# Float16 copies as 32-bit words on ScalarE, and a new written order, in a fused sliding-window attention and token-mixing kernel

## The chip, the cores and the metric

The kernel runs on one core of a Trainium2 chip. The metric is the device time of one execution in microseconds. Three runs of the kernel before took 137.32, 137.8 and 139.23 us; their median is 137.8.

A core has TensorE (PE), which multiplies matrices and writes its results to PSUM; VectorE (DVE) and ScalarE (ACT), which read PSUM and write SBUF; GpSimd (POOL), which here mostly issues the loads; and SyncE (SP), which here issues stores. The engines run side by side and wait for each other through semaphores.

## The reference

Eight batches, eight heads, 576 positions, head size 64. First causal attention over a window of 128 keys with a slope per head, then, with the heads laid side by side (512 columns), a mixing step over the tokens:

```python
scores = scale * np.matmul(q, k.transpose(0, 1, 3, 2))
rel = pos[:, None] - pos[None, :]
bias = slopes[:, None, None] * (-np.abs(rel))[None, :, :]
scores = np.where((rel >= 0) & (rel < 128), scores + bias[None], -1e9)
attn = softmax(scores)                       # over the keys
x = np.matmul(attn, v)                       # then (batch, 576, 512)
wq, wk = x @ w_q, x @ w_k                    # 512 -> 64
W_tok = np.einsum('bsd,btd->bst', wq, wk) / 8
mixed = np.einsum('bst,btd->bsd', W_tok, x)
out = np.maximum(mixed, 0.0) @ w_out         # float32
```

## The kernel before

Every piece of work is an operation with a name, a batch and a part. The long text `ORDER` lists all of them; the kernel issues them in exactly that order, and each word says on which engine the operation runs (`P`, `A`, `D`, `G`, `S` for PE, ACT, DVE, POOL, SP) and, for PE, which PSUM banks it writes. PSUM is used as four pairs of banks. Each engine executes its own operations strictly in the order of the text, so an operation that waits holds up all that is behind it on that engine.

Per batch b:

- `Lq`, `Lk`, `Lv`, `Lt` load q, k, v and the last 64 rows of q and k, converting to float16; POOL issues them. K comes in four parts of 128 rows (128 KB each as float16), Q of batches 1 to 4 in one load of 512 KB, Q of batches 5 to 7 in four loads of 128 KB, V in five parts. Three buffers hold K, two Q, four V, so a load waits until the batch that had its buffer is through. Batch 0's first blocks come in float32 through ACT and SP (`LF`).
- `TQ`, `TK`, `TT`, `TJ`, `TF` transpose q and k on PE by a product with an identity; `ETQ`, `ETK`, `ETT`, `EJ`, `EF` copy the result from PSUM to SBUF (tile qkT), on DVE or ACT as the order says.
- `QK b.g.u` computes the scores of 128 keys for half of the heads; `EXP` takes their exponential on ACT into tile pt (64 of them in all); `MUL` on DVE multiplies by the precomputed exp(bias), zero outside the window.
- `PV b.t` multiplies with V, which has a column of ones beside each head, so that the sums of the exponentials come with it; `RC` and `X` on DVE take the reciprocal and scale (tile x). `ones` sets that column in each of the four V buffers (tile vt) before the first load.

Two batches form a group for the mixing step: `XT`, `XTT` transpose x on PE and `EXT`, `EXTT` copy it out (tiles xT, xTt); `WQ`, `WK`, `WT`, `G` are products, evicted with conversion by `EWQ`, `EWK`, `EWT`, `EG`; `MX` and `RM`, `RMT` give the rectified mix (tile rm); `OUT` multiplies with w_out, `EO` copies to tile osb, `DO` stores.

`WM.i` are matmuls on a zeroed tile (tile warm) whose results nobody reads; `WARM` gives how many each one has. `bias`, `wmc`, `zeros`, `pads`, `ident`, `idh` prepare constants.

All copies from PSUM without arithmetic go through one helper, `cp`, in lines 250 to 254: `nc.scalar.copy` on ACT (line 252), `nc.vector.tensor_copy` on DVE (line 254). So in the profile all of these stand under L252 and L254, all products under L240, all transposes under L243; L657 is `EXP`, L672 `MUL`, L723 `RC`, L733 `X`, L886 and L888 are `RM` on ACT and DVE. Loads of K, Q and V are L367, L371 (L379 for batches 5 to 7) and L393.

Of the kernel before, what the change touches and what calls it, by code (L numbers as in the profile page):

```python
# [17 lines left out]
H = 8  # L18
# [36 lines left out]
EXP0.0.1:A QK0.2.1:P3 EJ0.1.1:D QK0.2.0:P2 QK0.1.1:P1 EXP0.2.1:A MUL0.0:D TQ1:P0 EXP0.2.0:A
Lv0.2:G QK0.1.0:P3 Lt0:G ETQ1:D EXP0.1.0:A TK1.0:P2 ETK1.0:D EXP0.1.1:A Lv1.0:G MUL0.2:D
WM.2:P01 QK1.1.1:P2 QK1.1.0:P3 QK1.0.1:P1 EXP1.1.1:A Lv1.1:G QK1.0.0:P0 MUL0.1:D EXP1.1.0:A
Lq2.0:G TK1.1:P2 ETK1.1:D EXP1.0.1:A Lk2.3:G PV0.0:P3 QK1.2.1:P2 RC0.0:D Lk2.2:G X0.0:D
EXP1.0.0:A PV0.1:P1 MUL1.1:D PV0.2:P3 Lv1.2:G EXP1.2.1:A QK1.2.0:P0 Lv0.3:G RC0.1:D EXP1.2.0:A
X0.1:D TT0:P2 RC0.2:D Lv1.3:G TJ0.3.1:P1 X0.2:D ETT0:A XT0.0:P00 ETT1:A MUL1.0:D Lk2.0:G  # L60
EJ0.3.1:A WM.3:P01 QK1.3.0:P2 Lv0.4:G EXP1.3.0:A EXT0.0:D PV1.0:P1 QK0.3.1:P3 RC1.0:D PV1.1:P0
X1.0:D EXP0.3.1:A QK0.3.0:P2 MUL1.2:D QK1.3.1:P1 EXP0.3.0:A TQ2:P3 Lk2.1:G RC1.1:D EXP1.3.1:A
MUL0.3:D Lv1.4:G ETQ2:A WM.4:P21 TK2.1:P1 X1.1:D Lt1:G ETK2.1:D PV1.2:P2 XT1.0:P00 RC1.2:D
PV0.3:P3 X1.2:D Lw1:G QK2.2.1:P1 MUL1.3:D Lk3.1:G EXP2.2.1:A Lw0:G RC0.3:D WM.5:P01 PV1.3:P2
EXT1.0:A X0.3:D Lq3.0:G PV0.4:P01 RC1.3:D X1.3:D TK2.0:P3 QK2.2.0:P1 Lv2.0:G RC0.4:D PV1.4:P00
ETK2.0:D EXP2.2.0:A XT1.1:P20 Lk3.0:G RC1.4:D X0.4:D QK2.0.0:P3 EXT1.1:D XT0.1:P21 EXP2.0.0:A
Lk3.3:G QK2.0.1:P1 X1.4:D EXT0.1:D QK2.1.1:P0 Lk3.2:G EXP2.0.1:A TT2:P3 QK2.1.0:P2 ETT2:D
Lv2.1:G EXP2.1.1:A ETT3:D WK0:P10 MUL2.0:D Lv2.2:G EXP2.1.0:A XTT0:P0 QK2.3.0:P3 EXTT0:D
WQ0:P11 Lv2.3:G EWK0:A MUL2.1:D EXP2.3.0:A QK2.3.1:P0 TQ3:P2 Lq4.0:G MUL2.2:D EXP2.3.1:A Lwo0:G
WT0:P10 ETQ3:D PV2.0:P0 EWT0:A Lwo1:G TK3.0:P3 ETK3.0:A G0:P10 RC2.0:D Lk4.1:G X2.0:D MUL2.3:D  # L70
EWQ0:A Lk4.0:G TK3.1:P3 EG0:A QK3.0.0:P0 EXP3.0.0:A Lv3.0:G ETK3.1:D MX0.0:P1 QK3.0.1:P2
RM0.0:D MX0.1:P3 EXP3.0.1:A Lv3.1:G MX0.3:P0 Lq5.01:G RM0.3:D RM0.1:A PV2.1:P1 QK3.1.0:P2
# [24 lines left out]
QK6.0.1:P3 ETT7:D DO2.1:S QK6.0.0:P1 ETQ7:D Lv6.3:G EXP6.0.1:A PV5.4:P20 DO0.1:S OUT3.2:P21
DO1.3:S Lv6.4:G EXP6.0.0:A RC5.4:D DO1.0:S MUL6.1:D QK6.3.0:P0 Lv7.0:G DO0.0:S PV5.3:P3
EXP6.3.0:A OUT3.1:P10 X5.4:D Lv7.4:G RC5.3:D EO3.2:A X5.3:D Lv7.2:G QK6.3.1:P0 EO3.1:A
QK7.1.0:P2 MUL6.0:D MX2.4:P3 EXP6.3.1:A XT5.1:P11 Lv7.1:G OUT2.0:P10 RMT2:D EXP7.1.0:A EXT5.1:D  # L100
TK7.1:P0 QK7.0.0:P3 EO2.0:A XTT4:P2 MUL6.2:D OUT3.0:P11 EXTT4:A EXP7.0.0:A ETK7.1:D WT4:P10
QK7.1.1:P2 MUL6.3:D EWT4:A QK7.0.1:P3 PV6.0:P0 EXP7.1.1:A WK4:P10 RC6.0:D X6.0:D EXP7.0.1:A
PV6.1:P2 MUL7.1:D PV6.2:P0 EO3.0:A QK7.3.0:P3 EWK4:A RC6.2:D DO3.0:S RC6.1:D WQ4:P11 X6.2:D
EXP7.3.0:A DO1.1:S X6.1:D PV6.4:P10 DO1.2:S EWQ4:A QK7.3.1:P0 DO2.3:S RC6.4:D QK7.2.1:P2 X6.4:D
QK7.2.0:P3 EXP7.3.1:A DO0.3:S MUL7.0:D G4:P11 DO1.4:S EXP7.2.1:A DO2.2:S MUL7.3:D PV6.3:P0
DO2.0:S EG4:A OUT3.4:P10 DO3.1:S EXP7.2.0:A RC6.3:D X6.3:D PV7.4:P11 EO3.4:A MX4.4:P2 MX4.1:P3
# [53 lines left out]
def kernel(  # L160
# [75 lines left out]
    def hold(i):  # L236
        held.append(i.ins)
# [12 lines left out]
    def cp(eng, out_ap, in_ap):  # L250
        if eng == "ACT":
            hold(nc.scalar.copy(out_ap, in_ap))  # L252
        else:
            hold(nc.vector.tensor_copy(out=out_ap, in_=in_ap))  # L254
# [820 lines left out]
```

## Time and profile before

| | |
|---|---|
| median of three runs | 137.8 us (137.32 to 139.23) |
| the profiled execution, its own time | 137.96 us |
| its span on the core | 135.9 us |
| mean granted TensorE clock | 0.982 |
| busy: PE / DVE / ACT / POOL | 122.4 / 114.2 / 107.4 / 86.4 us |
| first exponential starts, last one ends | 10.10, 105.42 us |
| last load issued by POOL | 93.2 us |

Each line of the views gives an engine, the kernel's line, the operation and its tiles as output<-input with shapes, then counts and times. Matmul ends are modelled in this profile, so a PE that is busy all the time may still contain short waits. "Idle before" is time in which an engine waited ahead of an instruction, with the engine and line that ended the wait.

### The profile page before, as it was taken

How to read it: one execution, taken by the hardware profiler on the slowest of the kernel's cores; microseconds unless marked ns; L12 is line 12 of the kernel's file. 1: busy time of each engine (PE TensorE's matmuls, PEld its weight loads, DVE VectorE, ACT ScalarE, POOL GpSimd, SP SyncE). 2: the span in 40 equal slices, each digit the busy share in tenths (PEclk: the TensorE clock that was granted, in tenths of full speed). 3: DMA queues.
4: the chain of work that ended last, by engine and by line, in shares of the span. 5: the costliest groups of instructions: out<-in, count | busy, mean ns of one | idle time of the engine just before them, and what ended most of it. 6: DMA issues, size and time to landing. Idle time of an engine off the chain costs nothing.

```text
span 135.9 us, 5044 instructions
## 1 busy us (share of the span) xinstructions
PE 122.4 (90%) x2169; PEld 78.1 (57%) x2169; DVE 114.2 (84%) x197; ACT 107.4 (79%) x145; POOL 86.4 (64%) x108
## 2 busy tenths in 40 slices
PE   6778778888999799999999999999999999999960
PEld 2356555765676476575566575565685576634430
DVE  5746699998999999998999999699999999557720
ACT  2579699985999999998999999999999953276040
POOL 7997979698989857999999999998000000000000
PEclk9997799999999999999999999999999999999997
DMA  4999999999999999999999999999999800958794
GB/s 91 214 176 171 157 154 181 164 159 151 148 164 160 197 186 154 157 154 157 155 157 158 152 150 155 154 192 265 226 244 376 306 20 0 299 187 312 236 378 138
DMA packets 105414, 24.97 MB, mean 184 GB/s; under 512 B 95536, under 2 KB 100912, under 8 KB 105392
## 3 DMA queue, kind: packets, MB, share of 16 engines
q0 software_dynamic: 96832, 14.42, 149.6%
q1 hardware_dynamic: 6688, 9.44, 20.6%
q10 hardware_dynamic: 1872, 0.79, 2.2%
q8 instruction: 17, 0.28, 0.8%
q14 instruction: 5, 0.04, 0.1%
HBM read 29.62 MB, written 9.44 MB: 287 GB/s over the span
## 4 chain that ended last, share of the span: by engine, by line
PE 57%; DMA 17%; DVE 8%; POOL 6%; ACT 6%; issue 3%; ACTq 0%; POOLq 0%; DVEq 0%
PE pair L240 48%; DMA natk<-in_k_dram 11%; PE pair L243 9%; DMA natq<-in_q_dram 6%; POOL natk L367 3%; ACT pt L657 3%; DVE pt L672 3%; DVE qkT L254 2%; DVE rm L888 1%; POOL vt L393 1%; POOL natq L371 1%; DVE x L733 1%; ACT rm L886 1%; ACT wqT L252 0%; ACT gs L252 0%
## 5 line engine op out<-in xcount | busy, mean ns | idle before, releaser
L657 ACT ACTIVATE pt<-pair 128x1024 f16<-128x1024 f32 x64 | 63.0, 1038 | 6.5 <-PE pair L240 5.9
L672 DVE TENSOR_TENSOR pt<-pt,bias 128x2048 f16<-128x2048 f16 x32 | 38.5, 1216 | 0.4 <-ACT pt L657 0.3
L393 POOL DMA_DIRECT2D vt<-in_v_dram x40 | 35.3, 968 | 2.2 <-DMA natk<-in_k_dram 1.0
L240 PE MATMUL pair<-wout_sb,rm 128*128 128x512 f16 (+1 forms) x132 | 31.7, 373 | 0.0
L367 POOL DMA_DIRECT2D natk<-in_k_dram x31 | 28.6, 946 | 1.7 <-DMA natq<-in_q_dram 1.4
L240 PE MATMUL pair<-qkT 64*128 64x256 f16 (+2 forms) x320 | 23.0, 256 | 1.3 <-DVE qkT L254 0.8
L240 PE MATMUL pair<-vt,pt 128*128 128x65 f16 (+1 forms) x576 | 22.1, 194 | 1.8 <-DVE rm L888 0.5
L240 PEld LDWEIGHTS <-pt 128*128 128x128 f16 (+1 forms) x576 | 19.2, 100 | 7.7 <-issue 3.4
L254 DVE COPY qkT<-pair 128x1024 f16<-128x1024 f16 (+2 forms) x27 | 19.3, 735 | 4.0 <-PE pair L243 3.9
L733 DVE TENSOR_TENSOR x<-pair,inv 128x512 f16<-128x512 f32 x32 | 21.8, 690 | 0.9
L252 ACT COPY osb<-pair 128x512 f32<-128x512 f32 (+1 forms) x24 | 14.0, 596 | 10.4 <-PE pair L240 5.1
L240 PEld LDWEIGHTS <-rm 128*128 128x128 f16 x132 | 11.4, 97 | 12.0 <-issue 2.2
L240 PEld LDWEIGHTS <-qkT 64*128 64x128 f16 x320 | 11.4, 95 | 8.9 <-issue 5.5
L254 DVE COPY osb<-pair 128x512 f32<-128x512 f32 (+1 forms) x13 | 8.7, 667 | 5.1 <-PE pair L240 5.1
L379 POOL DMA_DIRECT2D natq<-in_q_dram x12 | 11.5, 995 | 2.2 <-PE pair L240 1.8
L886 ACT ACTIVATE rm<-pair 128x1024 f16<-128x1024 f32 x11 | 11.1, 1045 | 0.5 <-PE pair L240 0.3
L243 PE MATMUL pair<-identh,x 128*128 128x128 f16 x128 | 9.9, 220 | 0.0
L243 PEld LDWEIGHTS <-x 128*128 128x128 f16 x128 | 7.5, 98 | 2.3 <-issue 1.3
L254 DVE COPY xT<-pair 128x1024 f16<-128x1024 f16 x11 | 7.5, 686 | 1.2 <-PE pair L243 1.1
L243 PE MATMUL pair<-identh,natk 64*128 64x64 f16 x248 | 6.7, 191 | 2.0 <-ACT qkT L252 0.7
L243 PEld LDWEIGHTS <-natk 64*128 64x128 f16 x248 | 5.5, 95 | 4.7 <-DMA natk<-in_k_dram 2.1
L243 PE MATMUL pair<-identh,natq 128*64 128x128 f16 (+2 forms) x256 | 7.8, 217 | 0.0
(68 smaller groups left out, 134.7 us busy)
## 6 DMA issues: line engine op xcount, KB each, us to landing
out_dram<-osb SPq DMA_DIRECT2D x30, 256.0 KB, 4.5
vt<-in_v_dram POOLq DMA_DIRECT2D x32, 128.0 KB, 6.7
natk<-in_k_dram POOLq DMA_DIRECT2D x31, 128.0 KB, 6.1
natq<-in_q_dram POOLq DMA_DIRECT2D x4, 512.0 KB, 7.5
natq<-in_q_dram POOLq DMA_DIRECT2D x12, 128.0 KB, 5.5
out_dram<-osb SPq DMA_DIRECT2D x9, 128.0 KB, 2.7
vt<-in_v_dram POOLq DMA_DIRECT2D x8, 64.0 KB, 5.9
natt<-in_q_dram POOLq DMA_DIRECT2D x4, 128.0 KB, 5.8
```

Of the source, the lines that this page charges most:

```text
L240: hold(nc.tensor.matmul(*a, **k))
L243: hold(nc.tensor.transpose(*a))
L252: hold(nc.scalar.copy(out_ap, in_ap))
L254: hold(nc.vector.tensor_copy(out=out_ap, in_=in_ap))
L367: return lambda: nc.gpsimd.dma_start(out=natk(b, n), in_=k[b, :, P * n:P * n + P, :].transpose([1, 0, 2]))
L371: return lambda: nc.gpsimd.dma_start(out=natq_s[b % NQ][r0 // QR:P].rearrange("p h r d -> p h (r d)"), in_=q[b, :, r0:512, :].rearrange("h ...
L379: return lambda: nc.gpsimd.dma_start(out=rows_q(b)[:, r], in_=q[b, :, 0:512, :].rearrange("h (p r) d -> r p h d", r=QR)[r])
L393: return lambda: nc.gpsimd.dma_start(out=vtv(b, t)[:n, :, 0:D], in_=v[b, :, P * t:P * t + n, :].transpose([1, 0, 2]))
L657: nc.scalar.activation(out=pt, in_=two(hold_.bank).rearrange("p e c -> p (e c)"), func=AF.Exp, scale=SCALE)
L672: nc.vector.tensor_tensor(out=pv, in0=pv, in1=bt, op=ALU.mult)
L733: nc.vector.tensor_tensor(out=x_s[b % NX][qt].rearrange("p (g h d) -> p g h d", g=2, h=4), in0=sums(p)[:, :, :, 0:64], in1=box["inv"].unsq ...
L886: hold(nc.scalar.activation(out=out_ap, in_=in_ap, func=AF.Relu, scale=WSCALE))
```

## The change

The helper `cp` looks at the types: where ACT copies float16 to float16 (all the transposes), both sides are seen as 32-bit words of two values each. The column of ones of V buffer 1 is no longer set by DVE: DVE writes one word (1.0 and 0.0) in a small tile, and ACT copies it to all 40 places. And the text `ORDER` and the counts in `WARM` are new: 694 operations in place of 693 (one more group of warm matmuls), 29 warm matmuls in place of 17.

```diff
-WARM = (6, 4, 1, 1, 2, 3,)
+WARM = (12, 3, 1, 6, 1, 3, 3,)
 
 ORDER = """
-warm:D LF0.0.0.0:A LF0.0.1.0:S ones.2:D iota:G LF0.0.1.1:A LF0.1.0.0:S ident:G LF0.0.0.1:A
...
+warm:D iota:G LF0.0.0.0:A LF0.0.1.0:S ones.0:D WM.0:P31 ident:G LF0.0.1.1:A LF0.1.0.0:S ones.2:D
...
     def cp(eng, out_ap, in_ap):
         if eng == "ACT":
+            if out_ap.dtype == F16 and in_ap.dtype == F16:
+                out_ap, in_ap = out_ap.bitcast(FP32), in_ap.bitcast(FP32)
             hold(nc.scalar.copy(out_ap, in_ap))
         else:
             hold(nc.vector.tensor_copy(out=out_ap, in_=in_ap))
...
-    sets = [add("ones", "", i, -58 + 10 * i, DVE(0.65), [], lambda o, t=t: mk_ones(t)) for i, t in enumerate(vt_s)]
+
+    onep = cpool.tile([P, 2], F16, name="onep")
+
+    def mk_onep(t):
+        nc.vector.memset(onep[:, 0:1], 1.0)
+        nc.vector.memset(onep[:, 1:2], 0.0)
+        nc.vector.memset(t[64:128, 4], 0.0)
+        nc.scalar.copy(
+            t.rearrange("p t h w -> p (t h) w")[:, :, D:D + 2].bitcast(FP32),
+            onep.bitcast(FP32).unsqueeze(1).broadcast_to([P, 5 * H, 1]))
+
+    sets = [add("ones", "", i, -58 + 10 * i, DVE(0.65), [], lambda o, t=t, i=i: mk_onep(t) if i == 1 else mk_ones(t))
+            for i, t in enumerate(vt_s)]
```

Which engine makes the copies changes with the order:

| copies | ACT before | ACT after | DVE before | DVE after |
|---|---|---|---|---|
| ETQ, 2048 values a partition | 1 | 4 | 6 | 3 |
| ETK, 1024 | 1 | 7 | 13 | 7 |
| EXT, 1024 | 5 | 9 | 11 | 7 |
| ETT and EXTT, 512 | 5 | 6 | 7 | 6 |
| EJ (batch 0) | 1 | 0 | 3 | 4 |
| EWQ, EWK, EG (float32 to float16, 512) | 11 | 4 | 1 | 8 |
| RM, 1024 | 11 | 13 | 5 | 3 |
| EO, 512 float32 (halves counted as one) | 24 | 25 | 13 | 12 |
| EF (batch 0, float32 to float16) | 2 | 4 | 2 | 0 |

Three places of the order. First ACT where batch 1 ends and batch 2 begins. Before (pt_102 here is batch 2's first pair of exponentials, the copies to qkT_76 are Q and K of batch 2):

```order
L657 ACTIVATE pt_99<-pair_141 128x1024
L252 COPY qkT_76<-pair_143 128x4x512
L657 ACTIVATE pt_102<-pair_141 128x1024
L252 COPY xT_123<-pair_140 128x4x256
L657 ACTIVATE pt_102<-pair_141 128x1024
L657 ACTIVATE pt_100<-pair_143 128x1024
```

and in the change, where pt_100 is batch 2's first pair:

```order
L251 COPY qkT_76<-pair_141 128x2x4x2x32
L668 ACTIVATE pt_99<-pair_143 128x1024
L251 COPY xT_123<-pair_142 128x4x128
L251 COPY qkT_76<-pair_140 128x4x256
L668 ACTIVATE pt_100<-pair_140 128x1024
L668 ACTIVATE pt_100<-pair_142 128x1024
L668 ACTIVATE pt_101<-pair_140 128x1024
```

The copies there have half as many elements, a K copy is among them, and the batch starts with the first block of keys in place of the third.

Second, POOL's loads of the same time. Before (natq_78 is Q of batch 2; natk_88 to natk_91 its K parts 0 to 3; vt_94 and vt_95 V of batches 0 and 1):

```order
L371 DMA natq_78<-in_q_dram 128x8x256
L367 DMA natk_91<-in_k_dram 128x8x64
L367 DMA natk_90<-in_k_dram 128x8x64
L393 DMA vt_95<-in_v_dram 128x8x64
L393 DMA vt_94<-in_v_dram 128x8x64
L393 DMA vt_95<-in_v_dram 128x8x64
L367 DMA natk_88<-in_k_dram 128x8x64
L393 DMA vt_94<-in_v_dram 64x8x64
L367 DMA natk_89<-in_k_dram 128x8x64
```

and in the change:

```order
L378 DMA natk_88<-in_k_dram 128x8x64
L404 DMA vt_94<-in_v_dram 128x8x64
L404 DMA vt_95<-in_v_dram 128x8x64
L404 DMA vt_94<-in_v_dram 128x8x64
L378 DMA natk_89<-in_k_dram 128x8x64
L382 DMA natq_78<-in_q_dram 128x8x256
L404 DMA vt_95<-in_v_dram 128x8x64
L404 DMA vt_94<-in_v_dram 64x8x64
L378 DMA natk_90<-in_k_dram 128x8x64
L378 DMA natk_91<-in_k_dram 128x8x64
```

K parts 0 and 1 and one V load of batch 0 (the second vt_94) now stand ahead of Q; before, they stood behind it. K parts 2 and 3 have moved the other way.

Third, DVE where batch 2 ends and batch 3 begins. Before (pt tiles are batch 2's; the copies to qkT_77 are the tail and Q of batch 3):

```order
L254 COPY qkT_77<-pair_143 128x8x64
L672 TENSOR_TENSOR pt_100<-pt_100,bias 128x2048
L254 COPY xTt_126<-pair_140 128x512
L672 TENSOR_TENSOR pt_101<-pt_101,bias 128x2048
L672 TENSOR_TENSOR pt_102<-pt_102,bias 128x2048
L254 COPY qkT_77<-pair_142 128x4x512
L723 RECIPROCAL inv<-pair_140 128x8
L733 TENSOR_TENSOR x_112<-pair_140,inv 128x512
```

and in the change:

```order
L253 COPY qkT_77<-pair_142 128x8x64
L738 TENSOR_TENSOR xtl_120<-pair_143,invt 128x256
L253 CAST wqT_128<-pair_143 128x512
L253 COPY xTt_126<-pair_141 128x512
L683 TENSOR_TENSOR pt_101<-pt_101,bias 128x2048
L683 TENSOR_TENSOR pt_103<-pt_103,bias 128x2048
L683 TENSOR_TENSOR pt_102<-pt_102,bias 128x2048
L734 RECIPROCAL inv<-pair_142 128x8
L744 TENSOR_TENSOR x_112<-pair_142,inv 128x512
```

The copy of batch 3's Q has left DVE, and a conversion of wqT has come to it.

More of the change, by code (lines that the diff above doesn't have):

```diff
@@ L55 @@
[L55 to L60, printed above, removed]
@@ L115 @@
[L115 to L117 removed]
+warm:D iota:G LF0.0.0.0:A LF0.0.1.0:S ones.0:D WM.0:P31 ident:G LF0.0.1.1:A LF0.1.0.0:S ones.2:D
+LF0.0.0.1:A LF0.1.0.1:S wmc:D Lv2.4:G Lq0.2:G Lk0.2:G pads:D bias:A ones.1:D Lk0.1:G ones.3:D
+Lq1.0:G idh:D zeros:D Lk1.1:G TF0.1.1:P00 TF0.1.0:P01 TF0.0.1:P10 Lk1.0:G EF0.1.0:A TF0.0.0:P11
```

123 lines of the change are left out of this document (62 added, 61 removed).

## The prediction

> **What bounds the kernel now.** I read the page's engine totals first, then the busy time by stretch, then the chain that ended last, and last the groups by form, which give prices. The stretches (columns: us, then PE, weight load, DVE, ACT and POOL busy with counts, granted clock, DMA share, GB/s):
>
> ```profile
> span 135.9 us, 5044 instructions
> PE 122.4 (90%) x2169; PEld 78.1 (57%) x2169; DVE 114.2 (84%) x197; ACT 107.4 (79%) x145; POOL 86.4 (64%) x108
> ...
> 0.00:17.00 17.00, 12.76 (x151) 7.72 (x152) 10.21 (x28) 11.04 (x17) 15.25 (x25) 0.90 1.63 162
> 17.00:31.00 14.00, 11.65 (x260) 8.65 (x257) 13.60 (x22) 12.78 (x16) 11.47 (x15) 1.00 2.24 164
> 31.00:41.00 10.00, 9.25 (x219) 6.54 (x219) 9.30 (x18) 8.69 (x10) 9.37 (x11) 1.00 2.01 155
> 41.00:55.50 14.50, 13.34 (x274) 8.74 (x270) 14.33 (x22) 13.76 (x20) 11.39 (x15) 1.00 2.04 173
> 55.50:78.00 22.50, 22.18 (x442) 14.32 (x442) 21.45 (x35) 21.41 (x31) 22.44 (x27) 1.00 2.43 156
> 78.00:105.40 27.40, 27.28 (x567) 17.98 (x567) 25.95 (x43) 26.71 (x38) 16.44 (x20) 1.00 1.95 220
> 105.40:131.00 25.60, 25.60 (x281) 14.10 (x280) 18.96 (x34) 12.47 (x19) 0.00 (x0) 1.00 0.61 209
> ```
>
> No one engine bounds the whole. Up to 55.5 us PE has gaps (1.2 to 4.2 us a stretch); from there to 131 us it has 0.4 us of gaps in 75.5 us, with ACT and DVE at 95% or more until 105.4. POOL, which issues the loads, is full from 55.5 to 78. The chain says who was late where:
>
> ```profile
> PE 57%; DMA 17%; DVE 8%; POOL 6%; ACT 6%; issue 3%; ACTq 0%; POOLq 0%; DVEq 0%
> ...
> 9.58 8.42 DMA natk<-in_k_dram
> ...
> 18.55 7.56 DMA natq<-in_q_dram
> ...
> 26.71 6.70 DMA natk<-in_k_dram
> ...
> 36.85 0.76 DVE qkT L254 x2
> ...
> 47.53 0.70 DVE x L733
> ```
>
> Loads hold most of the chain to 33.4 us, DVE nearly all from 36.9 to 48.2, PE (57% of the span) most of the rest. So a cheaper copy can earn only before about 55 us; after that it meets PE, and the loads behind it.
>
> **The change, part by part.** Prices first, by form (busy, mean ns):
>
> ```profile
> L252 ACT COPY xT<-pair 128x1024 f16<-128x1024 f16 x5 | 5.1, 1026 | 0.0
> L252 ACT COPY qkT<-pair 128x512 f16<-128x512 f16 x4 | 2.2, 655 | 0.2 <-DVE qkT L254 0.2
> L252 ACT COPY qkT<-pair 128x2048 f16<-128x2048 f16 x1 | 1.9, 1872 | 0.0
> L252 ACT COPY xTt<-pair 128x512 f16<-128x512 f16 x2 | 1.2, 590 | 0.0
> L252 ACT COPY qkT<-pair 128x1024 f16<-128x1024 f16 x1 | 1.0, 1012 | 0.1
> L252 ACT CAST gs<-pair 128x512 f16<-128x512 f32 x4 | 2.4, 612 | 1.5 <-PE pair L240 1.5
> L252 ACT COPY osb<-pair 128x512 f32<-128x512 f32 x23 | 13.6, 605 | 9.7 <-PE pair L240 5.1 <-DMA out_dram<-osb 4.6
> L252 ACT COPY osb<-pair 128x256 f32<-128x256 f32 x1 | 0.4, 373 | 0.7 <-DVE osb L254 0.7
> L657 ACT ACTIVATE pt<-pair 128x1024 f16<-128x1024 f32 x64 | 63.0, 1038 | 6.5 <-PE pair L240 5.9
> L254 DVE COPY qkT<-pair 128x1024 f16<-128x1024 f16 x14 | 9.5, 686 | 1.1 <-PE pair L243 1.1
> L254 DVE COPY osb<-pair 128x512 f32<-128x512 f32 x12 | 8.3, 688 | 3.6 <-PE pair L240 3.6
> L254 DVE COPY qkT<-pair 128x2048 f16<-128x2048 f16 x6 | 7.3, 1219 | 1.6 <-PE pair L243 1.6
> L888 DVE TENSOR_SCALAR rm<-pair 128x1024 f16<-128x1024 f32 x5 | 6.0, 1216 | 0.0
> ```
>
> A 1024-value f16 copy becomes 512 words. No row shows f16 as words; the same engine, source and word count is osb's 128x512, so I take 0.605 us (bounds: 0.373, the 256-word row, and 1.026, nothing saved). Likewise 2048 values take the 1024-element exponential's 1.038, 512 values 0.373.
>
> A rule against the change: the Trainium skill, "ScalarE: Activation LUTs", section "Rules for kernel authors", sends cheap element-wise work to VectorE, up to about three times faster per element. By it a moved 1024-value copy would cost 3 x 0.686 = 2.06 us (an estimate from that page's factor), and the 26 copies that ACT now gets, 27 x 1024 values a partition, 55.6 us. The trace disagrees even for unpacked values: 1.026 against 0.686, a factor of 1.5.
>
> ACT's f16 copies before: 5 x 1.026, 2 x 0.590, 4 x 0.655, 1.872, 1.012 = 11.8 us. After, 16 of 512 words (9 xT, 7 K), 4 of 1024 (Q), 6 of 256: 9.7 + 4.2 + 2.2 = 16.1. That is +4.3 for 13 more copies. Two more RM add 2.1 (an exponential's shape, 1.038 each), two more osb copies less a half one 0.8, two first-load casts 1.0 (by the osb rows of 512 and 256 words), seven f32 casts handed to DVE take 4.3 off, the ones add some 0.2 (bounds 0 and 0.373: it is 40 words). **ACT: +4.1 us.** DVE loses ten 1024-value copies (6.9), three of 2048 (3.7), two RM (2.4), small copies and casts net 2.1, and gains those seven casts at 0.69, as osb (4.8): **DVE: -10.2 us.** Together -6.1. By the order, from the first exponential to the last, ACT's sum stays (+0.3) and DVE's falls by 6.3; behind it ACT gets 2.6 more, DVE 2.4 less. What of this lies on the path:
>
> *Start, to 17 us.* Bias starts about 1 us sooner, since its DVE inputs come ahead of the zeros; but the first exponentials need all first casts, now four on ACT, and PE runs three warm matmuls ahead of the first QK and six ahead of QK0.1. The warm ones fill PE time up to the first loads.
>
> ```profile
> 12.76 1.92 PE L243 MATMUL pair<-identh,natq 128*64 128x128 f16 x32
> 26.39 1.08 PE L243 MATMUL pair<-identh,natq 128*64 128x128 f16 x32
> ...
> 124.25 7.08 PE L240 MATMUL pair<-wout_sb,rm 128*128 128x512 f16 x36
> ...
> 12.00:15.00 3.00, 3.00 (x44) 2.27 (x42) 1.50 (x2) 1.94 (x3) 2.26 (x4) 0.50 2.41 155
> ```
>
> The granted clock was 0.50 from 12 to 15, and the same Q transpose took 0.84 us longer than at full clock. If the fillers hold the clock, that pays for them: six matmuls of 512 columns at 0.20 (36 such in 7.08 us) are 1.2. The Trainium skill, "TensorE: Matmul & The Clock Gate", section "What's actually happening", has the clock halve after an idle window of some 3.4 us that runs free of the kernel; by it more fillers could win up to half of those 3 us, 1.5. I take 0 (bounds -0.8 and +1.2): loads, not PE, set the end of this stretch.
>
> *17 to 41 us, loads.* Batch 2's second K pair is what 26.71 + 6.70 = 33.41 in the chain is, and ACT shows the wait:
>
> ```profile
> 30.99 1.02 ACT L657 ACTIVATE pt<-pair 128x1024 f16<-128x1024 f32 x1 [1.06 <-PE pair L240]
> 31.91 1.01 ACT L252 COPY xT<-pair 128x1024 f16<-128x1024 f16 x1
> 34.06 1.02 ACT L657 ACTIVATE pt<-pair 128x1024 f16<-128x1024 f32 x1 [1.15 <-PE pair L240]
> ...
> natk<-in_k_dram POOLq DMA_DIRECT2D x31, 128.0 KB, 6.1
> natq<-in_q_dram POOLq DMA_DIRECT2D x4, 512.0 KB, 7.5
> ```
>
> Counting the loads that stand ahead of each in POOL's order, with these sizes, the Q load landing at 26.11 is the end of 3136 KB and the K load at 33.41 of 4096: 131 KB/us. In the new order Q ends 3520 KB (384 more, 2.9 us: about 29.0) and the last K load of the batch 3968 (128 less, 1.0 us: about 32.4), its first K pair long before. So the first exponential of batch 2 comes near 29.0 + 1.1 (transpose) + 1.0 (Q copy, now 1.038 where ACT's took 1.872) + 0.4 (QK) = 31.5, 0.5 later than 30.99; the second no longer waits for 33.41. ACT has 1.3 us idle in 31 to 41; the batch ends as much sooner as its last load: **-1.0 us**.
>
> *41 to 55 us, DVE.* The Q copy of batch 3 (1.219) leaves it and a cast of wqT (0.69) comes: **-0.5 us**. ACT's 0.7 us of idle there must hold it; past that ACT is next.
>
> *55 to 131 us.* Total PE work is the same, PE has no gaps: 0. The loads cap any lead:
>
> ```profile
> L243 PE MATMUL pair<-identh,natq x32: 190/190/190, 88.5 to 89.0; 64*128 64x64 f16 x32
> ...
> L379 POOL DMA_DIRECT2D natq<-in_q_dram x8: 976/1049/1117, 66.3 to 81.6; - x8
> ...
> DMA to landing us min/median/max: 5.2/5.5/5.7
> ```
>
> The last Q part is issued at 81.6, landed 5.5 later at 87.1, and is transposed at 88.5: 1.4 us of slack, some more with the new load order (it stands 192 KB sooner). So a lead of 1.5 survives, one of 3 would not. In the tail one OUT and more RM move behind the last exponential: PE is full there either way, 0 (bounds -0.5 and +0.9, one OUT).
>
> Sum: 0 - 1.0 - 0.5 = -1.5 us from the profiled execution's own 137.96 us (span 135.9 and 2.1 around it): 136.5. That execution is 0.16 above the median of 137.8; I forecast **136.4**.
>
> **The rivals.** *Evictions bound everything (faster).* PE's ends are modelled, so its full stretches may hide waits for PSUM. Then half the 6.1 us saved on DVE and ACT together comes off, 3.0, and with the clock dip gone (0.84) 137.8 - 3.9 = 133.9. For it: ACT and DVE at 95%. Against: ACT's own sum does not fall, and the Q slack of 1.4.
>
> *Q of batch 2 comes too late (slower).* One mechanism: POOL's load order. The batch cannot begin before its Q load, 2.9 us later; if ACT has run out of older exponentials by then and later batches keep that distance, 137.8 + 2.9 - 0.5 = 140.2. It decides if batch 2's first exponential starts after about 33. Against: K comes sooner, and all of batch 0's and 1's exponentials stand ahead.
>
> *The words save nothing (slower).* If a word costs two values, 16.1 becomes about 27.6, 11.5 more on an ACT that has some 5 us of idle up to 105: 137.8 + 6 = 144.
>
> **How the numbers follow.** Forecast 0.50 (own range 135.2 to 138.0), faster rival 0.25, late Q 0.20, no saving 0.05. The range takes in the first three with their start bounds: 133.6 to 140.2. Two per cent is 2.8 us (135.0 and 140.6), about what a measurement of this kernel can tell from no change. Faster: the rival and a tip of the forecast, 0.26. Slower: no saving, and a third of late Q, 0.12. Within: 0.62.
>
> **What would show it.** Rows of xT and qkT on ACT as 128x512 f32 at 0.60; ACT near 111 us, DVE near 104; the first exponential of batch 2 near 31.5 with no wait of 1.1 behind it; PE without gaps from about 54; the last Q transpose near 87. I am wrong if those copies stay at 1.0 us, if PE waits for natq after 60 us, or if PE's full stretch itself shrinks by over 2 us.

## The result, and the profile after

The change makes the kernel a little slower. Over 20 executions each it takes 138.87 us (median; 138.52 to 139.32) where the kernel before takes 137.94 us (136.96 to 139.57): a ratio of 1.0085, 95% interval 1.0066 to 1.0104. The forecast was 136.4 us, faster; the sign was wrong, and the time lies inside the range of 133.6 to 140.2. Ratios compare with executions of the kernel before taken beside the run, and leave out those more than 1.5% above the fastest of their kernel, so that a ratio can differ a little from that of the medians given here. Where the two differ I give both; 0.001 of a ratio is 0.14 us.

The profiled execution took 139.06 us, with a span of 137.1 us. Its engine totals:

```profile
span 137.1 us, 5069 instructions
PE 124.9 (91%) x2181; PEld 79.0 (58%) x2181; DVE 105.8 (77%) x187; ACT 111.3 (81%) x157; POOL 86.1 (63%) x108
```

ACT has 3.9 us more and DVE 8.4 us less than before; the forecast said 4.1 more and 10.2 less. The prices of the copies, by form (L251 is now `cp` on ACT):

```profile
L251 ACT COPY xT<-pair 128x512 f32<-128x512 f32 x9 | 5.1, 594 | 1.6 <-PE pair L240 1.5
L251 ACT COPY qkT<-pair 128x512 f32<-128x512 f32 x7 | 4.2, 597 | 0.3 <-PE pair L240 0.3
L251 ACT COPY qkT<-pair 128x1024 f32<-128x1024 f32 x4 | 4.1, 1014 | 1.3 <-PE pair L240 1.2
```

A copy of 1024 float16 values takes 594 to 597 ns where it took 1026, one of 2048 takes 1014 in place of 1872. So the words do what the change says, at the forecast prices. The same stretches as before (columns: length, then PE, weight load, DVE, ACT and POOL busy with counts, granted clock, DMA share, GB/s):

```profile
0.00:17.00 17.00, 15.36 (x164) 7.84 (x166) 8.57 (x26) 12.89 (x21) 15.67 (x25) 1.00 1.67 162
17.00:31.00 14.00, 11.05 (x259) 8.34 (x253) 12.84 (x20) 12.49 (x17) 11.28 (x15) 1.00 2.25 163
31.00:41.00 10.00, 9.34 (x233) 6.96 (x231) 8.92 (x18) 9.40 (x13) 9.77 (x13) 1.00 2.04 168
41.00:55.50 14.50, 13.09 (x254) 8.30 (x250) 11.53 (x19) 13.33 (x18) 11.67 (x14) 1.00 2.10 170
55.50:78.00 22.50, 22.15 (x446) 14.93 (x446) 20.74 (x37) 21.40 (x30) 21.33 (x26) 1.00 2.39 163
78.00:105.40 27.40, 26.90 (x552) 18.12 (x549) 25.07 (x41) 25.86 (x37) 16.40 (x20) 1.00 1.95 219
105.40:131.00 25.60, 25.54 (x290) 13.73 (x289) 17.34 (x31) 15.01 (x25) 0.00 (x0) 1.00 0.53 177
```

From 41 us on DVE is less busy in every stretch, by 2.80, 0.71, 0.88 and 1.62 us, and PE is less busy too: by 0.25, 0.03, 0.38 and 0.06. PE's idle time from 41 to 131 us is 90.0 - 87.68 = 2.32 us in after and 90.0 - 88.40 = 1.60 before. To see how far the work had come, I take the first product of each pair of batches that needs all of that pair's x (`G`), and PE's last piece. Before, and then after (columns: start, length):

```profile
42.22 1.05 PE L240 MATMUL pair<-x,wk 128*64 128x512 f16 x8
74.15 1.05 PE L240 MATMUL pair<-x,wk 128*64 128x512 f16 x8
102.33 1.05 PE L240 MATMUL pair<-x,wk 128*64 128x512 f16 x8
118.21 1.03 PE L240 MATMUL pair<-x,wk 128*64 128x512 f16 x8
125.77 5.57 PE L240 MATMUL pair<-wout_sb,rm 128*128 128x512 f16 x29
```

```profile
41.78 1.05 PE L237 MATMUL pair<-x,wk 128*64 128x512 f16 x8
74.80 1.05 PE L237 MATMUL pair<-x,wk 128*64 128x512 f16 x8
102.38 1.05 PE L237 MATMUL pair<-x,wk 128*64 128x512 f16 x8
119.23 1.05 PE L237 MATMUL pair<-x,wk 128*64 128x512 f16 x8
125.73 6.70 PE L237 MATMUL pair<-wout_sb,rm 128*128 128x512 f16 x34
```

The first is 0.44 us earlier, the second 0.65 later, the fourth 1.02 later, and PE ends at 132.43 in place of 131.34, 1.09 later. Of that, 0.72 is the idle time behind 41 us. The other 0.37 is counted as busy (89.11 us behind 41 us in place of 88.74), but it is not more work: 1536 matmuls start behind 41 us in after and 1544 before, and by their rows and columns they come to the same within 0.1%. Since the ends of matmuls are modelled, it is time in which PE waited inside stretches that look full. So at 41 us PE had done no more than before, and the whole 1.09 us is lost behind 41 us. The span grew by 1.2.

The stretch in which I forecast the gain shows it on ACT, and only there. Around the first exponentials of batch 2:

```profile
30.59 1.01 ACT L251 COPY qkT<-pair 128x1024 f32<-128x1024 f32 x1 [0.69 <-PE pair L240]
32.09 3.77 ACT L668 ACTIVATE pt<-pair 128x1024 f16<-128x1024 f32 x4 [0.48 <-PE pair L237]
...
36.46 3.78 ACT L668 ACTIVATE pt<-pair 128x1024 f16<-128x1024 f32 x4
```

They start at 32.09 (forecast 31.5; 30.99 before) and run on without the wait of 1.15 for K; the last ends at 40.24, where it was 39.36 + 2.00 = 41.36 before:

```profile
39.36 2.00 ACT L657 ACTIVATE pt<-pair 128x1024 f16<-128x1024 f32 x2
```

That is 1.1 us sooner, as forecast. On DVE, in the stretch where I forecast another 0.5, the time saved has become waits for PE:

```profile
43.97 0.21 DVE L734 RECIPROCAL inv<-pair 128x8 f32<-128x8 f32 x1 [1.28 <-PE pair L237]
...
47.58 1.22 DVE L899 TENSOR_SCALAR rm<-pair 128x1024 f16<-128x1024 f32 x1 [1.54 <-PE pair L237]
```

PE's own longest waits in this stretch have moved from DVE to ACT. Before, and then after:

```profile
45.18 0.61 PE L240 MATMUL pair<-wqT,gs 64*128 64x512 f16 x4 [0.29 <-DVE qkT L254]
46.31 0.64 PE L240 MATMUL pair<-vt,pt 128*128 128x65 f16 x16 [0.52 <-DVE rm L888]
```

```profile
45.58 0.75 PE L240 MATMUL pair<-identh,natq 128*64 128x128 f16 x20 [0.33 <-ACT pt L668]
48.30 0.64 PE L237 MATMUL pair<-vt,pt 128*128 128x65 f16 x16 [0.39 <-ACT qkT L251]
```

With the shorter ones, of 0.23 us for ACT before, of 0.26 for ACT and 0.29 for nothing that the trace shows in after, DVE ends 0.81 of 1.04 us before and ACT 0.98 of 1.27 us in after. The waits for ACT return in the other runs that keep after's order in this stretch.

### The profile page after: what moved, and what is told of

Same layout as the page of the kernel before. It is cut to its first block, busy times and chain, and to the rows that moved or that the text cites. A ratio compares the mean times of both kernels' runs of the same rounds, so it can differ in the third digit from the quotient of the medians.

```text
span 137.1 us, 5069 instructions
## 1 busy us (share of the span) xinstructions
PE 124.9 (91%) x2181; PEld 79.0 (58%) x2181; DVE 105.8 (77%) x187; ACT 111.3 (81%) x157; POOL 86.1 (63%) x108
## 4 chain that ended last, share of the span: by engine, by line
PE 69%; ACT 10%; DVE 9%; issue 4%; DMA 3%; SPq 1%; DVEq 0%; ACTq 0%
PE pair L237 55%; PE pair L240 14%; ACT pt L668 7%; DMA osb<-in_q_dram 3%; DVE pt L683 3%; DVE x L744 3%; ACT qkT L251 2%; DVE qkT L253 2%; SPq L423 1%; DVE inv L734 1%; DVE xT L253 1%; ACT gs L251 0%; ACT xT L251 0%; DVE osb L253 0%; DVE xtl L738 0%
## 5 line engine op out<-in xcount | busy, mean ns | idle before, releaser
L404 POOL DMA_DIRECT2D vt<-in_v_dram x40 | 34.4, 870 | 4.3 <-DMA vt<-in_v_dram 2.1
L378 POOL DMA_DIRECT2D natk<-in_k_dram x31 | 27.8, 909 | 3.0 <-DMA natq<-in_q_dram 1.7
L251 ACT COPY osb<-pair 128x512 f32<-128x512 f32 x25 | 14.3, 606 | 8.9 <-PE pair L237 8.9
L253 DVE COPY qkT<-pair 128x1024 f16<-128x1024 f16 (+2 forms) x18 | 12.0, 670 | 7.1 <-PE pair L240 6.9
L897 ACT ACTIVATE rm<-pair 128x1024 f16<-128x1024 f32 x13 | 12.8, 1043 | 0.4 <-PE pair L237 0.2
L251 ACT COPY qkT<-pair 128x512 f32<-128x512 f32 (+2 forms) x15 | 9.7, 651 | 2.2 <-PE pair L240 1.6
L253 DVE COPY osb<-pair 128x512 f32<-128x512 f32 (+1 forms) x12 | 7.7, 643 | 4.6 <-PE pair L237 4.2
L390 POOL DMA_DIRECT2D natq<-in_q_dram x12 | 10.7, 897 | 0.9 <-PE pair L237 0.8
L237 PE MATMUL pair<-warm 128*128 128x512 f16 x29 | 9.8, 475 | 1.2 <-DVE warm L294 1.2
L734 DVE RECIPROCAL inv<-pair 128x8 f32<-128x8 f32 x32 | 6.4, 203 | 3.4 <-PE pair L237 2.9
```

The costliest lines, as they stand in the source:

```text
L237: hold(nc.tensor.matmul(*a, **k))
L378: return lambda: nc.gpsimd.dma_start(out=natk(b, n), in_=k[b, :, P * n:P * n + P, :].transpose([1, 0, 2]))
L390: return lambda: nc.gpsimd.dma_start(out=rows_q(b)[:, r], in_=q[b, :, 0:512, :].rearrange("h (p r) d -> r p h d", r=QR)[r])
L404: return lambda: nc.gpsimd.dma_start(out=vtv(b, t)[:n, :, 0:D], in_=v[b, :, P * t:P * t + n, :].transpose([1, 0, 2]))
L734: nc.vector.reciprocal(out=box["inv"], in_=sums(p)[:, :, :, 64])
L897: hold(nc.scalar.activation(out=out_ap, in_=in_ap, func=AF.Relu, scale=WSCALE))
```

## The experiments

### Words and order apart

*Only the words, in before's order.*

```diff
         if eng == "ACT":
+            if out_ap.dtype == F16 and in_ap.dtype == F16:
+                out_ap, in_ap = out_ap.bitcast(FP32), in_ap.bitcast(FP32)
             hold(nc.scalar.copy(out_ap, in_ap))
```

> The order and the fillers of before, with one edit: float16 copies on ACT as 32-bit words. Its 13 copies get shorter by 5 x 0.43 + 2 x 0.22 + 4 x 0.28 + 0.86 + 0.42, about 5.0 us of ACT. Theory (the words help, the new order costs): 0.5 to 1.5 us faster than before, with xT copies on ACT at 0.60. Rival (PE and the loads bound everything, copies are off the path): within 0.3 us of before.

Measured: 137.87 us (137.13 to 139.92), ratio 0.9965 (0.9924 to 1.0006). Its page:

```profile
PE 122.5 (89%) x2169; PEld 78.0 (57%) x2169; DVE 114.2 (83%) x197; ACT 103.5 (75%) x145; POOL 86.3 (63%) x108
```

ACT is relieved of 3.9 us (the run of the same order with more fillers, below, has 103.2). By the ratio the time falls by some 0.5 us, not clear of zero, which leaves both expectations open.

*Only the order, without the words* (the same two lines taken out of after).

> The change without the words: its order, fillers and the ones of one V buffer stay, float16 copies on ACT are made value by value again. 26 copies get longer by about 10.5 us of ACT in all. Theory (ACT is full up to the last exponential in the new order): 3 to 6 us slower than the change. Rival (PE bounds): less than 1.5 us slower than the change.

Measured: 147.42 us, ratio 1.0666 (1.0621 to 1.071).

```profile
PE 125.6 (86%) x2181; PEld 80.5 (55%) x2181; DVE 106.9 (73%) x187; ACT 122.3 (84%) x157; POOL 86.1 (59%) x108
```

ACT has 11.0 us more than in after, and 8.0 (by the ratios) to 8.5 (by the medians) appear in the time, more than either expectation allowed. So the new order cannot live without the words: in it they are worth some 8 us, in the old one about 0.5, not clear of zero. A copy's price seems to count where its engine has no room.

### Two guesses on the new order

*Batch 4's Q transpose and its copy some 20 operations later* (after has them early, ahead of batch 3's first exponentials).

```diff
-... EXP3.1.0:A TQ4:P3 Lk4.0:G ... MX0.2:P0 ETQ4:A TK3.1:P1 ...
+... EXP3.1.0:A Lk4.0:G ... MX0.2:P0 TK3.1:P1 ... OUT0.1:P20 TQ4:P3 X2.4:D ... QK3.2.0:P0 ETQ4:A Lk5.1:G ...
```

> The change, with one move: the transpose of batch 4's Q and its copy stand some 20 operations later, behind batch 3's second pair of exponentials, as in before. Theory (in the new order this copy holds up batch 3's exponentials and DVE between 43 and 50 us): 0.4 to 0.9 us faster than the change, no wait of 1.5 us of DVE ahead of RM near 47 us. Rival (the time lost there is made up later, or is lost elsewhere): within 0.3 us of the change.

Measured: 140.89 us, ratio 1.0185 (1.0146 to 1.0225), slower than after: the early place was not the loss, and neither expectation held. In the kept trace the clock fell in this stretch:

```profile
41.00:55.50 14.50, 12.95 (x250) 8.57 (x244) 11.10 (x17) 11.57 (x17) 12.05 (x15) 0.88 2.09 171
```

That is a small part of it: the executions of this run with a mean clock of 0.994 to 0.997 took 140.34 to 140.67 us as well.

*Fewer fillers* (`WARM = (12, 1, 1, 1, 1, 1, 1,)` in after).

> The change with 12, 1, 1, 1, 1, 1, 1 warm matmuls in place of 12, 3, 1, 6, 1, 3, 3: 11 fewer, some 2.3 us of PE between 9 and 22 us. Theory A (the fillers stand in the way): 0.5 to 1.5 us faster than the change. Theory B (they keep the clock up and loads set the pace there): no faster, and with the granted clock down to 0.5 for some 3 us, 0 to 1 us slower.

Measured: 139.75 us, ratio 1.0112 (1.007 to 1.0155), which overlaps after's; the granted clock is 1.00 in all seven stretches here too. So the fillers in between do not stand in the way (theory A falls); whether they earn something cannot be told from these intervals.

### Six copies moved from one engine to the other

In after, ETQ3, ETQ4, ETQ5, ETK5.1, ETK6.1 and ETK7.1 go back from ACT to DVE (`ETQ3:A` becomes `ETQ3:D`, and so on).

> After, with six word copies given back to DVE where they stand (ETQ3, ETQ4, ETQ5, ETK5.1, ETK6.1, ETK7.1): ACT 3.6 us less, DVE 4.1 us more. Theory (ACT is what PE waits for behind 42 us in the new order): 137.8 to 138.5 us, and EXP7.2.1 ends 0.5 to 1.0 us earlier than in after. Rival (the loss is not in the share of ACT but in the positions of the order): 138.8 us or more, since DVE gets what ACT loses.

Measured: 141.97 us, ratio 1.0285 (1.0252 to 1.0319).

```profile
55.50:78.00 22.50, 21.66 (x422) 14.15 (x416) 21.12 (x36) 19.12 (x25) 22.44 (x28) 1.00 2.39 163
78.00:105.40 27.40, 25.82 (x534) 17.71 (x534) 25.79 (x44) 24.61 (x35) 15.84 (x19) 1.00 1.95 216
```

In these 50 us ACT is relieved of 3.5 us, DVE is 1.1 us busier, and PE loses 1.57 us against after. The theory's time (137.8 to 138.5) is missed by far, and the time fits the rival. But the run does not clear ACT: it loads DVE by what it takes from ACT, and no run takes work from ACT alone in the new order.

The mirror image: before's order with words, the same six from DVE to ACT.

> Before's order with word copies, and the same six copies moved from DVE to ACT where they stand: DVE 4.1 us less, ACT 3.6 us more, so about as full as before the words. Theory of my prediction (the DVE's copies at 41 to 55 us and later hold PE up): 137.0 to 137.5 us, 0.4 to 0.8 less than with words alone (137.87). Rival (ACT is the engine PE waits for, and DVE's time is hidden): 138.0 to 138.8 us, the gain of the words spent again.

Measured: 139.61 us, ratio 1.0122 (1.0081 to 1.0162), 1.7 us (by the ratios 2.2) above words alone and above both expectations.

```profile
55.50:78.00 22.50, 21.49 (x420) 13.99 (x419) 18.84 (x32) 21.05 (x32) 22.15 (x27) 1.00 2.41 155
```

DVE has 3.7 us of room in this stretch, and PE is 0.69 us less busy than before. So handing DVE's copies to ACT does not give what my forecast expected of less DVE time. In either order, moving these six copies costs.

### Where in the program the new order loses

Two orders can be joined: the words of one up to some operation, then those of the other that are not yet in. The joint itself may cost.

*Old start, new rest* (joined behind batch 2's last exponential, 41 us):

```diff
 ... EWK0:A MUL2.1:D EXP2.3.0:A
-QK2.3.1:P0 TQ3:P2 Lq4.0:G MUL2.2:D EXP2.3.1:A ...
+Lq4.0:G EWQ0:D QK2.3.1:P2 EXP2.3.1:A WT0:P31 TQ3:P2 ...
```

> The word copies throughout (16 fewer instructions' worth of ACT time is not touched), the order of before up to the end of batch 2's exponentials (41 us), the order of after behind it; V ones by DVE and the filler counts as before. Theory (the loss is spread over 42 to 106 us, where the new order holds ACT nearly full): about as slow as after, 138.5 to 139.0 us. Rival (the loss comes from the new start, its load order and its late batch 2): the gain of the words alone, 137.5 to 138.0 us.

Measured: 142.36 us, ratio 1.0298 (1.0251 to 1.0345). PE stood waiting for a load, 2.36 us at 48.73 for Q of batch 4.

The new rest uses batch 4's Q earlier than the old start has loaded it, so this run says nothing on the rest.

*New start, old rest* (the same joint, the other way).

> The mirror image: the order of after up to the end of batch 2's exponentials, the order of before behind it, with word copies throughout. Theory (loss behind 42 us): 137.3 to 138.1 us, and if the new start gives anything this is the fastest of all, below 137.5. Rival (loss in the new start): 138.6 to 139.2 us.

Measured: 139.19 us, ratio 1.0091 (1.0059 to 1.0124), and again a load at the joint: PE waits 1.02 us at 44.90 for K of batch 3.

*The same with that load moved* up on POOL:

```diff
-... EXP2.2.1:A Lq4.0:G QK2.3.0:P0 EWQ0:D QK2.3.1:P2 Lk3.2:G ...
+... EXP2.2.1:A Lk3.2:G Lq4.0:G QK2.3.0:P0 EWQ0:D QK2.3.1:P2 ...
```

> The kernel with the new start and the old rest (139.19 us), in whose trace PE waited 1.02 us at 44.90 for a K load of batch 3, with that load put ahead of Lq4.0 on POOL. Theory (the new start gives nothing and costs nothing in PE progress; the load wait was the joint's own): 137.9 to 138.4 us. Rival 1 (the new start costs 1 us by itself): 138.9 us or more. Rival 2 (the new start is worth the 1 us that I forecast, hidden by that wait and others): below 137.5 us.

Measured: 138.08 us (137.49 to 138.61), ratio 1.0009 (0.998 to 1.0038). Of the joints at 41 us this is the one without a load wait, and its time lies where the theory put it. The new start, with its loads, its fillers and its earlier end of batch 2 on ACT, is worth nothing that can be seen (words with the old start: 0.9965; the intervals overlap, and the middles lie 0.6 us apart the wrong way). After's interval lies wholly above this one's: **a loss of 0.8 us by the medians, 1.0 by the ratios, comes behind 41 us.**

In the kept traces part of this loss lies behind PE's last product. Here PE ends at 124.87 + 7.08 = 131.95 and the span at 136.0, 4.1 us later; in after it is 132.43 and 137.1, 4.7 us later:

```profile
124.87 7.08 PE L236 MATMUL pair<-wout_sb,rm 128*128 128x512 f16 x36
```

So about 0.6 of the 1.1 us between these two spans falls where only the last copies and stores are left. The six kept traces with the new start and before's tail have 4.0 to 4.1 us there, the nine with after's tail 4.5 to 4.8, one of them 5.4. But before itself has 4.5, so against before the tail explains only 0.2. No run takes the tails apart.

I tried to place the loss by four more joints: after up to 58, 73, 80 or 106 us and the old order behind, and once the old order from 41 to 58 us only.

```diff
 ... XT3.0:P31 PV3.3:P2 MUL4.1:D
-EXT2.0:A TK5.0:P0 EXT3.0:A Lv4.2:G QK4.0.0:P1 ...
+EXT2.0:A Lv5.0:G EXT3.0:A RC3.3:D X3.3:D QK4.0.0:P1 TK5.0:P3 ...
```

> After up to 58 us (the two orders have then issued the same operations but for three on either side), before's order behind it; words throughout. With the new order throughout it is 138.87, with the new start to 41 us and the old rest 138.08. If the loss arises at 41 to 58 us: 138.7 to 139.1. If behind 58 us: 137.9 to 138.3. Half each: near 138.5.

> The mirror image: the new start with its K load of batch 3 earlier, before's order from 41 to 58 us, after's order behind 58 us. If the loss arises at 41 to 58 us: 137.9 to 138.3. If behind 58 us: 138.7 to 139.1. Half each: near 138.5.

> After up to 73 us, before's order behind it. In 55.5 to 78 us PE is idle 0.35 us in after and 0.32 in before, so the stretch from 58 to 73 should add nothing: as e13, within 0.2 us. If this one is 0.5 us or more above e13, the stretch from 58 to 73 is where the loss arises after all.

> After up to batch 6's query transposes (80 us), the order of before behind it, all copies as words. PE stood idle 0.50 us in 78 to 105.4 us of after and 0.12 in before. Theory (that 0.38 us is order, and the tail's 0.1 too): 138.2 to 138.6 us, 0.3 to 0.6 below after. Rival (the loss is all done by 80 us and later idle time only hands it on): 138.8 to 139.2 us.

> After up to its last exponential (106 us), the order of before behind it: PE's tail gets back the output product that after moved behind the exponentials only as far as it was already done, so the same work with the old copies and stores. Theory (the loss lies at 41 to 105 us, by PE's idle time 0.25 + 0.03 + 0.38 us more than before, and 0.06 behind): 138.6 to 139.0 us. Rival (the tail's copies and stores cost what is lost): 138.0 to 138.4 us.

Measured:

| run | us | ratio (95%) | PE waited at the joint |
|---|---|---|---|
| new to 58, then old | 139.69 | 1.0115 (1.0061 to 1.0169) | 0.56 and 0.40 us at 63 |
| old from 41 to 58, else new | 140.51 | 1.0188 (1.0136 to 1.0239) | three times 0.3 us, 62 to 71 |
| new to 73, then old | 139.64 | 1.0129 (1.0083 to 1.0176) | 0.74 us for V at 75.6 |
| new to 80, then old | 141.06 | 1.0199 (1.0136 to 1.0262) | 0.60 and 1.11 us at 82 to 84 |
| new to 106, then old | 139.94 | 1.0145 (1.0094 to 1.0196) | 1.53 us at 107 for x on DVE |

All five medians lie above those of both whole orders, and none in the range that a theory gave for it (only that joints at 58 and at 73 us give the same came true). Splitting the loss this way fails: each seam opens waits of its own, as the last column shows.

### The clock dip at the start

Before had the clock at 0.50 from 12 to 15 us. Here the old order with words gets more fillers:

```diff
-WARM = (6, 4, 1, 1, 2, 3,)
+WARM = (12, 4, 1, 1, 2, 3, 6,)
-... QK0.2.0:P2 QK0.1.1:P1 ...
+... QK0.2.0:P2 WM.6:P01 QK0.1.1:P1 ...
```

> Before's order with word copies and more filler products where PE is idle at the start (12 instead of 6 in the first, and 6 more ahead of QK0.1.1), so that the granted clock doesn't fall to 0.50 at 12 to 15 us. Theory (the dip costs PE little, since PE then waits for copies and exponentials anyway): 137.4 to 137.9 us, the times closer together. Rival (the dip costs its 1.5 us of lost PE speed): 136.3 to 136.8 us. Against both, if the fillers stand in the way of the first scores: 138.2 us or more.

Measured: 138.28 us (136.5 to 139.85), ratio 0.9957 (0.991 to 1.0004), the same as words alone.

```profile
0.00:17.00 17.00, 13.47 (x159) 7.57 (x161) 10.02 (x28) 10.97 (x17) 15.28 (x25) 1.00 1.64 162
```

The dip is gone (1.00 in place of 0.90) and nothing measurable is won: PE is idle for 3.5 us of that stretch anyway. (Words alone had the dip later in their kept trace, 0.88 from 17 to 31 us.)

### Work taken away

Since no joint could place the loss, the last runs ask what the kernel is bound by behind 41 us: they leave work out and change no order.

*Half of the bias products of batches 3 to 7*, in the old order with words and in after:

```diff
-            nc.vector.tensor_tensor(out=pv, in0=pv, in1=bt, op=ALU.mult)
+            m = P if b < 3 else P // 2
+            nc.vector.tensor_tensor(out=pv[:, :, :, 0:m], in0=pv[:, :, :, 0:m], in1=bt[:, :, :, 0:m], op=ALU.mult)
```

> Before's order with word copies, and the bias products of batches 3 to 7 made over half of their columns only (the other half of the weights stays without the bias): 20 instructions of DVE at about 0.63 instead of 1.22 us, some 11.5 us less DVE behind 41 us. Left out of the computation: half the bias products of those batches. Theory (PE is the bound behind 41 us, idle there 1.6 us in 90): at most 1.6 us faster than 137.87, I expect 136.7 to 137.4. Rival (copies and products on DVE set the pace, as the terms of my prediction for 17 to 55 us supposed): 2 us or more faster, below 135.9.

> After with the same half of the bias products left out for batches 3 to 7. If after's loss behind 41 us is PE's waits on copies and products: within 0.4 us of e16, 136.7 to 137.6. If the loss is in PE's own order, its sequencer's gaps or the tail: 0.8 us or more above e16, 137.8 to 138.5.

Measured: 137.77 us, ratio 0.9958 (0.9922 to 0.9994), and 138.69 us, ratio 1.0051 (1.0018 to 1.0083). A half product takes 0.68 us on DVE in place of 1.22. The old order's page, then after's:

```profile
PE 123.7 (91%) x2169; PEld 78.8 (58%) x2169; DVE 104.7 (77%) x197; ACT 103.2 (76%) x145; POOL 86.2 (63%) x108
```

```profile
PE 124.2 (91%) x2181; PEld 79.0 (58%) x2181; DVE 96.5 (71%) x187; ACT 111.3 (82%) x157; POOL 86.1 (63%) x108
```

DVE loses 9.5 and 9.3 us. By the ratios the time falls by 0.1 us in the old order, less than I expected, and by 0.5 in after (by the medians 0.1 and 0.2), and with and without the half products the intervals overlap. The two runs, taken side by side, are still 0.9 us apart by the medians and 1.3 by the ratios, as I expected for a loss in PE's own order, in gaps without a releaser or in the tail. So DVE's work behind 41 us is hardly on the path in either order, and most of after's loss is not waits on it. PE's visible idle time does not measure the loss either: from 41 to 131 us it is 1.66 us in this run of after's order and 1.62 in that of the old one.

*One of the four products per output tile of batches 0 to 3*, in after:

```diff
-            for db in range(4):
+            for db in (0, 2, 3) if b < 4 else range(4):
```

> After, with one of the four accumulated products left out of each output tile of batches 0 to 3 (18 products of 128x512, all but one of them issued between 46 and 105 us). Left out of the computation: a quarter of the last product of those tiles. By the profile one takes 0.248 us (124 of them 30.7 us): 18 x 0.248 = 4.5 us. Theory (PE's own stream is the bound behind 41 us, idle there 2.3 us in 90): 134.4 to 136.0 us, 2.9 to 4.5 less than after's 138.87. Rival (PE, ACT and DVE are chained so closely that ACT or DVE takes over as soon as PE gets shorter): 136.5 to 138.0 us, at most half of it comes back.

Measured: 139.5 us, ratio 1.0112 (1.0064 to 1.0159): nothing is won, which neither theory allowed. Its page:

```profile
PE 123.0 (89%) x2163; PEld 78.0 (57%) x2163; DVE 105.7 (77%) x187; ACT 111.1 (81%) x157; POOL 86.1 (63%) x108
```

The 4.5 us expected was too high a price: back to back a product takes 0.197 us (34 in 6.70), 3.5 us for 18. And PE's busy time falls by 1.8 us only, from 124.9 to 123.0, so that some 1.7 us of the time taken out is still counted as busy: PE's full stretches hold waits. What became of the time, by `G` of the second and third pair, and by the first product of batch 7 with its last V blocks:

```profile
75.11 1.05 PE L237 MATMUL pair<-x,wk 128*64 128x512 f16 x8
101.55 1.05 PE L237 MATMUL pair<-x,wk 128*64 128x512 f16 x8
...
110.24 1.12 PE L237 MATMUL pair<-vt,pt 128*128 128x65 f16 x32 [0.58 <-DMA vt<-in_v_dram]
```

```profile
55.50:78.00 22.50, 21.37 (x433) 14.36 (x433) 20.86 (x37) 21.39 (x30) 21.81 (x26) 1.00 2.38 162
```

Up to 78 us less work only made PE idle more (22.50 - 21.37 = 1.13 us, 0.35 in after), with ACT as busy as in after (21.39 and 21.40): the second `G` comes no sooner (75.11, 74.80). At 102 us 0.83 has been won, and at 110 us PE waits for V. POOL's V loads from 90 us on, in this run and in after (first and last start, then the time to landing):

```profile
L404 POOL DMA_DIRECT2D vt<-in_v_dram x7: 715/915/945, 89.6 to 94.4; - x7
...
DMA to landing us min/median/max: 9.1/9.6/15.7
```

```profile
L404 POOL DMA_DIRECT2D vt<-in_v_dram x7: 705/905/935, 89.4 to 94.6; - x7
...
DMA to landing us min/median/max: 9.2/9.9/15.1
```

```profile
110.36 1.13 PE L237 MATMUL pair<-vt,pt 128*128 128x65 f16 x32
```

In these traces the slowest load is the last one: it lands at 94.4 + 15.7 = 110.1 here, where PE's wait ends, and at 109.7 in after, 0.7 us ahead of its use at 110.36. In before the last is issued at 93.2 and lands 9.9 later, at 103.1, 6 us ahead of that product's start at 109.16:

```profile
L393 POOL DMA_DIRECT2D vt<-in_v_dram x6: 1010/1198/1227, 89.3 to 93.2; - x6
...
DMA to landing us min/median/max: 8.6/9.6/9.9
```

So in these two executions the last third has a floor that before has not: whatever gets PE to 110 us sooner by more than 0.7 us waits there. It is not a matter of the load order alone: with the same order on POOL, the last load took 13.3 us in the run of after with half products and 9.4 in that with six copies back on DVE.

## Why the prediction was wrong

*Prices, busy sums: right.* The copies (forecast 0.605 and 1.038, measured 0.595 and 1.014), ACT's sum (+4.1 and +3.9), DVE's (-10.2 and -8.4, some 2 too much) and the first exponential of batch 2 (31.5 and 32.09) came out near enough.

*Start, 0: right.* The dip went, and the run that removes it from the old order shows that its end is worth nothing that can be seen there.

*17 to 41 us, -1.0: the step that failed first.* I read "the batch ends as much sooner as its last load" on ACT, and on ACT it did (41.36 to 40.24). The step that failed is the next one, from ACT's lead to a lead of the kernel, for which I gave no row: at 41 us PE had done no more of its work than before, and right behind it DVE waited 1.28 and 1.54 us for PE. The last Q transpose, which I put near 87 us, starts at 88.8, and at 88.5 before. The new start by itself measures 1.0009 where words with the old start measure 0.9965. So the term measures nothing, or a loss of some tenths, where I wrote -1.0.

*41 to 55 us, -0.5: failed in the same way.* The chain of before was "DVE nearly all from 36.9 to 48.2", and I took a copy off DVE for time off the path. DVE's 2.8 us less in that stretch became idle time in front of PE, PE's own idle time there rose by 0.25, and most of it now ends with ACT, 0.98 of the 1.27 us shown above: "past that ACT is next" stood in my text, but no term did. Taking 9.5 us from DVE behind 41 us in the old order won 0.1. The chain names who came last at each step; it does not say how far behind the next one was.

*55 to 131 us, 0: this is where, with 41 to 55, the loss lies.* The run with the new start and the old rest puts 0.8 to 1.0 us behind 41 us. PE ends 1.09 us later for the same work: 0.72 us of it are idle time that the trace shows, 0.37 are hidden in busy time. Part of the 0.72 is a gap of 0.47 us in which the trace shows nothing that PE waited for:

```profile
99.48 0.73 PE L237 MATMUL pair<-vt,pt 128*128 128x65 f16 x18 [0.47 <-issue]
```

Such a gap comes and goes. The run with the old tail has after's order up to 106 us, and there PE is busy almost throughout:

```profile
78.00:105.40 27.40, 27.29 (x553) 18.20 (x550) 25.49 (x43) 26.49 (x37) 16.26 (x20) 1.00 1.96 223
```

The run with few fillers shows one of 0.92 us, the run of after with half products none of 0.2 us or more behind 50 us. So the gap is not settled as the order's doing. What returns is the difference at 41 to 55.5 us: PE is busy 13.08 and 13.09 us there in the runs with the old tail and with after's half products, 13.33 and 13.34 in those of the old order with more fillers and with half products. "Total PE work is the same, PE has no gaps: 0" was wrong as an argument as well: PE's full stretches hold waits, as the 18 products show, so they are no floor. In after, 18 products less on PE, 9 us less on DVE, and in the old order 4 us less on ACT each left the time where it was, within 0.5 us. None of these engines alone bounds it; ACT alone was not tried in the new order.

*The rivals.* "Evictions bound everything" had the right doubt, that PE's full stretches may hide waits, but its gain fell: the time rose, and the half products took 9.5 us from DVE for 0.1. "Q of batch 2 comes too late" named its condition (a first exponential after about 33) and it was not met (32.09); the new load order, with the rest of the new start, measures as neutral. "The words save nothing" fell with the rows at 594 ns. That the measured time lies in the range is luck: the range reached up to 140.2 for the late Q, which did not happen, and no rival had the loss that came.

*What stays open.* The 0.8 to 1.0 us is the new order behind 41 us, and its cause is open. Batch 4's early Q, the fillers and the six copies tried are not it, and DVE's work is half of it at most. What the runs leave is ACT, for which PE waits at 41 to 55 us (giving copies back costs 3, but loads DVE), the tail behind PE's last product, and waits hidden in PE's busy time. Which of the order's places loses it was not found; the late landing of the last V blocks is shown as a floor, but PE does not wait there in after itself.

## What to carry to other kernels

Where three engines and the loads are all busy for 90% or more, time saved on one is worth what the next can use of it, often nothing, while time added to one costs at once: 4 us less on ACT won 0.5 at best, moving six copies cost 1.7 or 3.1. Ask of each saved microsecond who waits for its end and how far behind the next bound is, and measure that by leaving work out before an order is rewritten around it. A full engine in a profile with modelled ends is no floor until taking work from it has shown it. And these orders could not be judged in pieces: every joint of the two had a median above both, except one where the loads had been put right.

## What was not expected of the hardware

The granted clock fell after a short gap. In the run with the old order from 80 us (columns as in the stretches above):

```profile
82.00:84.00 2.00, 0.40 (x8) 0.32 (x8) 1.06 (x2) 1.40 (x2) 2.00 (x4) 1.00 1.85 186
84.00:86.00 2.00, 1.97 (x44) 1.50 (x43) 0.89 (x2) 0.00 (x0) 1.68 (x3) 0.63 2.38 148
86.00:88.00 2.00, 2.00 (x8) 0.50 (x8) 1.97 (x4) 1.02 (x1) 2.00 (x3) 0.52 2.41 153
```

PE was idle 1.6 us in two, with eight matmuls in between, and then, if the clock is either whole or half, ran at half clock for some 3.4 us (0.37 x 2.0 and 0.48 x 2.0, doubled). The Trainium skill, "TensorE: Matmul & The Clock Gate", section "What's actually happening", has windows of about 3.4 us; the length of the dip agrees. It puts an idle window ahead of the throttle; here 1.6 us of idle time, in a stretch otherwise full, was enough. Not every such gap brings a dip: the wait of 1.53 us at 107 in the run with the old tail left the clock at 1.00 from 105.4 to 131 us.

The last V loads took up to 15.7 us to land, in after 15.1, where the median over all of after's V loads of that size is 7.2 (its page). From 90 to 110 us the output stores, 256 KB each, are in flight on the same DMA engines; that they are the cause was not tested.
